# A state-space mixer and an MLP on one core: tap products of single channels for two of four channel groups

## The chip, the core and the metric

The kernel runs on one NeuronCore of a Trainium2 chip. The core has a matrix engine (PE, with its weight loads shown as PEld), two engines that work on elements (DVE and ACT), a general one (POOL) and a queue engine that starts transfers (SP); ACT starts transfers too. PE writes only to PSUM, eight banks of 512 fp32 columns, which DVE or ACT must copy out. The metric is device time in microseconds of one execution; lower is better.

## What is computed

The input is 2048 positions of 512 channels. A layer norm feeds a diagonal state-space layer, which is a long convolution along the positions, one kernel of 2048 taps for each channel; the result is added to the input. A second layer norm feeds an MLP with 1376 hidden units, and its result is added too. Cut to what matters here:

```
P = exp(logdA[:, :, None] * l[None, None, :])          # logdA = dt * (A_re + i A_im), 512 x 128
K = einsum("dn,dnl,dn->dl", Cc, P, dB).real            # the taps: 512 channels x 2048
y = irfft(rfft(pad(u)) * rfft(pad(K)))[..., :L]        # causal convolution
h = x + y + u * Dskip                                  # u = layernorm(x)
h2 = h + gelu(layernorm(layernorm(h)) @ w1 + b1) @ w2 + b2
```

The position index `l` is in bf16, so positions above 256 fall together on multiples of 2, 4 and 8. The kernel therefore needs the taps only at a few distinct positions, and writes each as a product of two powers: one of 20 rows (`ROWS`, `NA = 20`) times one of 33 columns (`NB = 33`).

## The kernel before

**Tables.** The 512 channels are four groups `c` of 128 (`CW`). For each group there are four tables in SBUF with the 128 states on the partitions: `EA[c]`, `IA[c]` (cosine and sine part of the row powers with the coefficients) and `EB[c]`, `IB[c]` (of the column powers). `bexps` and `aexps` make the magnitudes on ACT, `chain` and `chain1` the phases: PE sums them up in PSUM, ACT takes the sine (L1026, L1063), DVE multiplies (L1036, L1043, L1068). A table keeps four channels side by side, so neighbouring rows of one channel lie four elements apart. The row tables have 32 rows (`NP_`) for each channel, of which 20 are used; `gap` (L756) clears the other twelve.

**Tap products.** `kgen(c)` (L1075 to L1104) makes the taps. One product takes two channels at once: its stationary operand is 52 wide (32 rows of one channel, then 20 of the next), its moving operand is 66 wide (33 columns of each). Of the four blocks that come out, the two on the diagonal are the channels' own taps and the other two are not used. Two column tiles of the array, `t` = 0 and 1, hold channels of the two halves. For each of 32 steps `i` there are four products in the order tile 0 real, tile 0 imaginary, tile 1 real, tile 1 imaginary; the imaginary one is added to the real one in PSUM. Five blocks of steps (7, 7, 7, 7, 4) fill banks, and three copies (`evac`: L616 on ACT, L618 on DVE) bring them to SBUF, blocks 1 and 2 together, 3 and 4 together, and 5. A small add (L1104) puts in `Dskip`. A group has 128 products.

**After the taps.** `kspec` (groups 0 and 1 together), `kspec1` (groups 2 and 3, one by one) and `ktail` (late positions) multiply the taps into the first stage of a Fourier transform (L1120, L1145, L1166), copy them out, and turn them by a transfer to DRAM and back; `fstage` (L967) does the second stage. The input goes through `lnorm`, `austage` (L946) and `fstage` in the same way, for two halves of the positions, b = 0 and 1. `inverse` multiplies spectra on DVE (L1235) and transforms back on PE (L1245). `tail` adds the result to the residual (L1319, L1322), takes statistics (L1323, then small steps on DVE with a power on POOL, L689, L694) and normalises (L1334, L1336); a transpose on PE (L1346) or by transfer follows. `mlp` has two matmuls (L1362, L1378) with the GELU on ACT (L1364) between them and the last add on DVE (L1380), from which each tile goes out in two transfers of 64 partitions.

**The order.** Nothing is scheduled while the kernel runs: each engine works through its instructions in the order in which they were written, and waits where an operand is late. Every step is recorded as an operation with its engine, a cost and what it depends on. `ORDER` is a list of all of them, found by a search ahead of time: an entry is twice the operation's number, plus one where an operation that two engines can do is put on the second. A negative entry stands for four products that nobody reads. `SLOTS` gives the PSUM bank for each new PSUM tile in turn. The costs in the code serve that search and change nothing on the chip.

Of the kernel before, what the change touches and what calls it, by code (L numbers as in the profile page):

```python
# [15 lines left out]
P = 128  # L16
# [259 lines left out]
class VS(V):  # L276
# [51 lines left out]
]  # L328
SLOTS = "0124626046204620462406220246200626224606446426424602606426042060242042604206246240264024604620406240245651620426262341302560134076205472541326036260721452042067563414307136506437056253104574107423"


TURN = 450000


class Sched:
    def __init__(self):
        self.ops = []
        self.wr, self.rd = {}, {}
# [102 lines left out]
def kernel(ctx, tc, A_u, A_A_re, A_A_im, A_B_re, A_B_im, A_C_re, A_C_im, A_log_dt, A_Dskip,  # L441
# [963 lines left out]
    for c in (2, 3):  # L1405
        chain1(c, 5 + 0.25 * c)
        if c == 2:
            gap(IA[2:3], 5.95)
# [92 lines left out]
```

## Time and profile before

| | |
|---|---|
| three executions, median | 230.77 us (230.60 to 230.82) |
| the profiled execution, its own time | 230.71 us |
| its span, first to last instruction | 228.9 us |
| busy PE, DVE, ACT, POOL | 196.2, 173.5, 164.4, 14.6 us |
| L1092, tap products, 512 | 18.3 us, first at 57.1, last at 93.3 |

The page gives each engine's busy time and its share of the span, then the span in 40 slices of 5.7 us with the busy share of each in tenths, then the chain of work that ended last. Views of the trace group instructions by line and shape, cut the span into stretches, or list the instructions in order of time. In a group the columns are: line, engine, operation, output and input, shapes, count, busy time in us, mean length of one in ns, idle time of the engine ahead of them and what ended it. Matmuls overlap in the array, so the mean length of one (242 ns for L1092) is far above busy time over count.

### The profile page before, as it was taken

How to read it: one execution, taken by the hardware profiler on the slowest of the kernel's cores; microseconds unless marked ns; L12 is line 12 of the kernel's file. 1: busy time of each engine (PE TensorE's matmuls, PEld its weight loads, DVE VectorE, ACT ScalarE, POOL GpSimd, SP SyncE). 2: the span in 40 equal slices, each digit the busy share in tenths (PEclk: the TensorE clock that was granted, in tenths of full speed). 3: DMA queues.
4: the chain of work that ended last, by engine and by line, in shares of the span. 5: the costliest groups of instructions: out<-in, count | busy, mean ns of one | idle time of the engine just before them, and what ended most of it. 6: DMA issues, size and time to landing. Idle time of an engine off the chain costs nothing.

```text
span 228.9 us, 6859 instructions
## 1 busy us (share of the span) xinstructions
PE 196.2 (86%) x2974; PEld 113.6 (50%) x2981; DVE 173.5 (76%) x279; ACT 164.4 (72%) x203; POOL 14.6 (6%) x26
## 2 busy tenths in 40 slices
PE   7113886776999899999999769999999999999993
PEld 4102752233874479756566446654444434444452
DVE  7999778999897995779899989899957467113022
ACT  4999999999888997998997598593325405803800
POOL 2000300300010001200000030300000101000000
PEclk9999999999999999999999999999999999999998
DMA  5970191153006955486698991019340142051202
GB/s 154 191 145 6 53 234 41 51 159 127 6 3 118 227 145 146 131 180 158 175 243 164 258 227 67 3 33 218 72 93 21 29 101 69 11 126 44 63 21 70
DMA packets 43159, 25.09 MB, mean 110 GB/s; under 512 B 30197, under 2 KB 40697, under 8 KB 43130
## 3 DMA queue, kind: packets, MB, share of 16 engines
q1 hardware_dynamic: 41576, 22.72, 44.2%
q10 hardware_dynamic: 1554, 1.93, 2.7%
q8 instruction: 23, 0.38, 0.7%
q14 instruction: 6, 0.05, 0.1%
HBM read 14.13 MB, written 5.28 MB: 85 GB/s over the span
## 4 chain that ended last, share of the span: by engine, by line
PE 53%; ACT 26%; DVE 10%; DMA 4%; issue 4%; POOL 1%; ACTq 0%; SPq 0%; DVEq 0%; POOLq 0%
PE ps L1362 17%; PE ps L1378 17%; ACT ar L616 8%; PE ps L1092 7%; ACT ar L793 7%; ACT ar L1063 5%; ACT ar L991 4%; PE ps L1245 4%; DVE ar L1235 2%; DMA HL_d<-ar 2%; PE ps L946 2%; DMA ar<-AKc_d 2%; DVE ar L971 1%; DVE ar L1068 1%; ACT ar L701 1%
## 5 line engine op out<-in xcount | busy, mean ns | idle before, releaser
L616 ACT CAST ar<-ps 128x1024 bf16<-128x1024 f32 (+3 forms) x73 | 62.4, 917 | 10.8 <-PE ps L1245 5.3
L1364 ACT ACTIVATE ar<-ps,ar 128x512 bf16<-128x512 f32 (+1 forms) x44 | 27.6, 685 | 34.1 <-PE ps L1362 28.6
L1362 PE MATMUL ps<-ar 128*128 128x512 bf16 (+1 forms) x176 | 40.1, 379 | 0.1
L1378 PE MATMUL ps<-ar 128*128 128x512 bf16 (+3 forms) x181 | 39.8, 366 | 0.3
L1380 DVE TENSOR_TENSOR ar<-ps,ar 128x512 bf16<-128x512 f32 (+1 forms) x17 | 10.6, 652 | 26.7 <-issue 19.7
L1378 PEld LDWEIGHTS <-ar 128*128 128x128 bf16 (+1 forms) x187 | 17.9, 98 | 19.7 <-issue 0.7
L1362 PEld LDWEIGHTS <-ar 128*128 128x128 bf16 (+1 forms) x176 | 17.3, 100 | 20.2 <-issue 0.5
L618 DVE CAST ar<-ps 128x1024 bf16<-128x1024 f32 (+4 forms) x18 | 19.5, 1091 | 6.6 <-PE ps L1092 2.5
L1235 DVE TENSOR_TENSOR ar<-ar 128x2048 bf16<-128x2048 bf16 x20 | 24.0, 1218 | 0.5 <-ACT ar L616 0.3
L1245 PE MATMUL ps<-ar 64*128 64x128 bf16 x672 | 21.5, 216 | 1.9 <-DVE ar L1235 1.5
L1245 PEld LDWEIGHTS <-ar 64*128 64x128 bf16 x672 | 19.1, 94 | 6.5 <-issue 3.2
L1063 ACT ACTIVATE ar<-ps 128x1024 bf16<-128x1024 int16 x20 | 19.5, 1037 | 1.6 <-PE ps L1061 1.4
L1092 PE MATMUL ps<-ar 128*52 128x66 bf16 x512 | 18.3, 242 | 0.4 <-DVE ar L1068 0.4
L689 POOL TENSOR_TENSOR ar<-ar 128x4 f32<-128x4 f32 (+1 forms) x6 | 9.5, 1577 | 143.3 <-DVE ar L694 104.6
L1092 PEld LDWEIGHTS <-ar 128*52 128x52 bf16 x512 | 16.8, 128 | 2.7 <-issue 1.8
L946 PE MATMUL ps<-ar 128*32 128x512 bf16 x256 | 16.4, 381 | 1.0 <-DVE ar L931 0.9
L1026 ACT ACTIVATE ar<-ps 128x1024 bf16<-128x1024 int16 x16 | 15.9, 1035 | 0.4 <-PE ps L1018 0.3
L793 ACT ACTIVATE ar<-ar 128x1024 bf16<-128x1024 f32 x16 | 15.6, 1044 | 0.6 <-DVE ar L675 0.6
L1061 PE MATMUL ps<-ar 128*32 128x256 f16 (+1 forms) x256 | 12.9, 301 | 3.0 <-ACT ar L1063 2.8
L694 DVE SCALAR_TENSOR_TENSOR ar<-ar 128x4 f32<-128x4 f32 (+3 forms) x33 | 9.9, 305 | 6.4 <-POOL ar L689 5.4
L967 PE MATMUL ps<-ar 128*64 128x128 bf16 (+2 forms) x160 | 13.6, 298 | 0.9 <-ACT ar L616 0.9
L1068 DVE TENSOR_TENSOR ar<-ar 128x1024 bf16<-128x1024 bf16 x20 | 12.9, 682 | 0.6 <-ACT ar L1063 0.4
(83 smaller groups left out, 229.0 us busy)
## 6 DMA issues: line engine op xcount, KB each, us to landing
ar<-in_A_u_dram SPq DMA_DIRECT2D x16, 128.0 KB
ar<-in_A_u_dram SPq DMA_DIRECT2D x8, 256.0 KB
out_dram<-ar SPq DMA_DIRECT2D x30, 64.0 KB
ar<-in_B_w_dram SPq DMA_DIRECT2D x3, 344.0 KB
AK_d<-ar SPq DMA_DIRECT2D x2, 512.0 KB
AKc_d<-ar SPq DMA_DIRECT2D x4, 256.0 KB
ar<-tab_TP SPq DMA_DIRECT2D x1, 768.0 KB
ar<-AKc_d SPq DMA_DIRECT2D x3, 256.0 KB
```

The costliest lines, as they stand in the source:

```text
L616: act.copy(out_fn(), in_fn())
L618: dve.tensor_copy(out_fn(), in_fn())
L793: add("ACT", c_act(1024) + 0.03, lambda e, e0=e0: act.activation(free(EB0 // 2 + 4 * (16 - e0), [[8 * e0, 2], [4 * NB, NCH * CW // 4], [1, ...
L946: pe.matmul(pst(p)[32 * j:32 * j + 32, 512 * z:512 * z + 512], lhsT=BX.ap()[:, f0 + z, 16 - 16 * c:48 - 16 * c], rhs=src[2 * j + c].ap(), ...
L1026: add("ACT", c_act(1024), lambda e, p=p, sc=sc, cs=cs: act.activation(sc[cs].ap().rearrange("p c e d -> p (c e d)").rearrange("p (x e f) - ...
L1063: add("ACT", c_act(1024), lambda e, sc=sc: act.activation(sc.ap().rearrange("p z a b -> p (z a b)").rearrange("p (x a f) -> p a x f", a=4, ...
L1092: pe.matmul(o, lhsT=free(ta.lo // 2 + q * 4 * NP_ + f, [[4, NP_ + NA]]), rhs=free(tb.lo // 2 + q * 4 * NB + f, [[4, 2 * NB]]), start=ta is ...
L1235: dve.tensor_tensor(pq.ap().rearrange("p n d -> p (n d)"), a, b_, ALU.mult)
L1245: pe.matmul(pst(p)[:, 512 * h + 128 * k:512 * h + 128 * k + 128], lhsT=q.ap()[rows, x, :], rhs=TP[w].ap()[rows, f0 // 2 + k, :], start=(n ...
L1362: pe.matmul(pst(p)[:fs], lhsT=w1s[dc].ap()[:, fc * P:fc * P + fs], rhs=ybuf.ap().rearrange("p (t c) k -> p c t k", c=4)[:, dc], start=(dc ...
L1364: add("ACT", c_act(512, 1), lambda e, p=p, fc=fc, fs=fs: act.activation(hT.ap()[:fs, fc, :], pst(p)[:fs], ACT.Gelu_apprx_tanh, bias=b1_sb. ...
L1378: pe.matmul(pst(p)[:, c0:c1], lhsT=hT.ap()[:fs, fc, 128 * t:128 * t + 128], rhs=w2s[fc].ap()[:fs, c0:c1], start=(fc == 0), stop=(fc == NFC ...
```

## The change

For groups 0 and 1 the tap products stay those of two channels, but they go through the array in turn: the loop over the tiles `t` is inside that over the real and imaginary part, so the order is tile 0 real, tile 1 real, tile 0 imaginary, tile 1 imaginary.

For groups 2 and 3 a product takes one channel: 20 wide in the stationary operand and 33 in the moving one. Four column tiles `g` of 32 are used in turn, eight products a step, 256 a group. No unused blocks come out, so PSUM holds half as much: three blocks of steps (11, 11, 10) and two copies, of 726 and 330 elements for each partition, in place of three of 924, 924 and 264. The tap buffers `kgc` are half as large, `kspec1` and `ktail` read them without the index of the two channels, and the unused rows of `EA[2]`, `EA[3]` and `IA[2]` need no clearing: one `gap` on DVE and one on POOL go.

With that the program has 902 recorded operations instead of 914, and `ORDER` and `SLOTS` are new from the first entry to the last.

```diff
 ORDER = [
-    2, 0, 52, 4, 58, 54, 56, 50, 62, 154, 6, 64, 66, 68, 74, 82, 8, 102, 104, 12, 10, 136, 194, 14, 140, 106, 88, 108, 16, 24, 32, 118, 100, 60, 28,
...
-    1814, 1820, 1822, 1826, 1824,
+    52, 0, 6, 2, 50, 4, 8, 12, 10, 56, 62, 292, 22, 60, 152, 64, 100, 190, 66, 72, 84, 98, 14, 94, 134, 102, 58, 104, 16, 70, 162, 106, 116, 90, 68,
...
+    1798, 1800, 1802, 1774, 1758, 1752, 1776, 1784, 1786, 1778, 1788, 1760, 1790, 1762, 1764, -7, 1766,
 ]
...
-    kgc = [at(lo, bf16, 2, NB, 32) for lo in (xall.lo + 10240, K0)]
+    kgc = [at(lo, bf16, NB, 32) for lo in (xall.lo + 10240, K0)]
...
     gap(EA[0:2], 0, "DVE")
-    gap(EA[2:4], 0, "DVE")
...
-    KIS = [[(0, 7), (7, 7)], [(14, 7), (21, 7)], [(28, 4)]]
+    KIS2 = [[(0, 7), (7, 7)], [(14, 7), (21, 7)], [(28, 4)]]
+    KIS1 = [[(0, 11), (11, 11)], [(22, 10)]]
+    two = (0, 1)
...
-                    def fn(e, p=p, nb=nb, i0=i0, lo=lo, hi=hi):
+                    def fn2(e, p=p, nb=nb, i0=i0, lo=lo, hi=hi):
                         for i in range(lo, hi):
-                            for t in range(2):
-                                q, f = 16 * t + 2 * ((i0 + i) // 4), (i0 + i) % 4
-                                o = pst(p)[64 * t:64 * t + 32 + NA, 512 * nb + 2 * NB * i:512 * nb + 2 * NB * i + 2 * NB]
-                                for ta, tb in ((Ar, Br), (Ai, Bi)):
-                                    pe.matmul(o, lhsT=free(ta.lo // 2 + q * 4 * NP_ + f, [[4, NP_ + NA]]), rhs=free(tb.lo // 2 + q * 4 * NB + f, [[4, 2 * NB]]), start=ta is Ar, stop=ta is Ai, tile_position=(0, 64 * t))
-                    add("PE", 0.064 * (hi - lo), fn, r=[Ar, Br, Ai, Bi], w=[p], new=[p] if first else [])
+                            for ta, tb in ((Ar, Br), (Ai, Bi)):
+                                for t in range(2):
+                                    q, f = 16 * t + 2 * ((i0 + i) // 4), (i0 + i) % 4
+                                    o = pst(p)[64 * t:64 * t + 32 + NA, 512 * nb + 2 * NB * i:512 * nb + 2 * NB * i + 2 * NB]
+                                    pe.matmul(o, lhsT=free(ta.lo // 2 + q * 4 * NP_ + f, [[4, NP_ + NA]]), rhs=free(tb.lo // 2 + q * 4 * NB + f, [[4, 2 * NB]]), start=ta is Ar, stop=ta is Ai, tile_position=(0, 64 * t), skip_group_check=True)
+
+                    def fn1(e, p=p, nb=nb, i0=i0, lo=lo, hi=hi):
+                        for i in range(lo, hi):
+                            for ta, tb in ((Ar, Br), (Ai, Bi)):
+                                for g in range(4):
+                                    q, f = 16 * (g // 2) + 2 * ((i0 + i) // 4) + g % 2, (i0 + i) % 4
+                                    o = pst(p)[32 * g:32 * g + NA, 512 * nb + NB * i:512 * nb + NB * i + NB]
+                                    pe.matmul(o, lhsT=free(ta.lo // 2 + q * 4 * NP_ + f, [[4, NA]]), rhs=free(tb.lo // 2 + q * 4 * NB + f, [[4, NB]]), start=ta is Ar, stop=ta is Ai, tile_position=(0, 32 * g), skip_group_check=True)
+                    add("PE", (0.064 if Z == 2 else 0.074) * (hi - lo), fn2 if Z == 2 else fn1, r=[Ar, Br, Ai, Bi], w=[p], new=[p] if first else [])
...
-        add("DVE", c_dve(64), lambda e: dve.tensor_tensor(ks()[:, :, 0], ks()[:, :, 0], Dz.ap()[:, c, :].unsqueeze(1).to_broadcast([P, 2, 32]), ALU.add), r=[kg, Dz], w=[kg])
+        if Z == 2:
+            add("DVE", c_dve(64), lambda e: dve.tensor_tensor(ks()[:, :, 0], ks()[:, :, 0], Dz.ap()[:, c, :].unsqueeze(1).to_broadcast([P, 2, 32]), ALU.add), r=[kg, Dz], w=[kg])
+        else:
+            add("DVE", c_dve(32), lambda e: dve.tensor_tensor(ks()[:, 0], ks()[:, 0], Dz.ap()[:, c, :], ALU.add), r=[kg, Dz], w=[kg])
...
     for c in (2, 3):
         chain1(c, 5 + 0.25 * c)
-        if c == 2:
-            gap(IA[2:3], 5.95)
```

More of the change, by code (lines that the diff above doesn't have):

```diff
@@ L292 @@
 ORDER = [
[35 rows of a table removed]
[34 rows of a table added]
 ]
-SLOTS = "0124626046204620462406220246200626224606446426424602606426042060242042604206246240264024604620406240245651620426262341302560134076205472541326036260721452042067563414307136506437056253104574107423"
+SLOTS = "01426060264062402460202046022460606024202462442620402640202406264206426042604204624064026042642064023602546047020202637260670613216270324165464674304620431463172506156323475041273641671651307452"
 TURN = 450000
@@ L1078, in kgen @@
         kg = Kg[0] if c < 2 else kgc[c - 2]
-        ks = (lambda: kg.ap()[:, :, :, c]) if c < 2 else kg.ap
+        Z = 2 if c in two else 1
+        ks = (lambda: kg.ap()[..., c, :]) if c < 2 else kg.ap
+        KIS = KIS2 if Z == 2 else KIS1
         for grp in KIS:
@@ L1098, in ofn @@
             def ofn(i0=i0, n=n, N=N):
-                return ks().rearrange("p z k i -> p (z k) i")[:, :, i0:i0 + n * N].rearrange("p q (b i) -> p q b i", b=N)
+                a = ks()
+                if Z == 2:
+                    a = a.rearrange("p z k i -> p (z k) i")
+                return a[:, :, i0:i0 + n * N].rearrange("p q (b i) -> p q b i", b=N)
             def ifn(p=p, n=n, N=N):
-                return pst(p).rearrange("p (b q) -> p b q", b=N)[:, :, 0:2 * NB * n].rearrange("p b (i q) -> p q b i", q=2 * NB)
-            evac(ofn, ifn, 2 * NB * n * N, [p], [kg])
-        add("DVE", c_dve(64), lambda e: dve.tensor_tensor(ks()[:, :, 0], ks()[:, :, 0], Dz.ap()[:, c, :].unsqueeze(1).to_broadcast([P, 2, 32]), ALU.add), r=[kg, Dz], w=[kg])
+                return pst(p).rearrange("p (b q) -> p b q", b=N)[:, :, 0:Z * NB * n].rearrange("p b (i q) -> p q b i", q=Z * NB)
+            evac(ofn, ifn, Z * NB * n * N, [p], [kg])
+        if Z == 2:
+            add("DVE", c_dve(64), lambda e: dve.tensor_tensor(ks()[:, :, 0], ks()[:, :, 0], Dz.ap()[:, c, :].unsqueeze(1).to_broadcast([P, 2, 32]), ALU.add), r=[kg, Dz], w=[kg])
+        else:
+            add("DVE", c_dve(32), lambda e: dve.tensor_tensor(ks()[:, 0], ks()[:, 0], Dz.ap()[:, c, :], ALU.add), r=[kg, Dz], w=[kg])
     def kspec(q, pr):
@@ L1144, in mm @@
                         oo = pst(ps[g // 2])[:, 512 * (g % 2) + 256 * cp:512 * (g % 2) + 256 * cp + 256].rearrange("p (k i) -> p k i", k=8)
-                        pe.matmul(oo, lhsT=W.ap()[rows, tl, P * v:P * v + P], rhs=kg.ap()[rows, g % 2, k0:k0 + 8, :], start=(m == 0), stop=(m == len(js) - 1), tile_position=(32 * g, 0))
+                        pe.matmul(oo, lhsT=W.ap()[rows, tl, P * v:P * v + P], rhs=kg.ap()[rows, k0:k0 + 8, :], start=(m == 0), stop=(m == len(js) - 1), tile_position=(32 * g, 0))
             add("PE", 0.45 * (1 + cp), mm, r=[kg, W], w=ps, new=ps if cp == 0 else [])
@@ L1156, in ktail @@
         al = ALb[q]
-        kk = (lambda x: Kg[0].ap()[:, :, :, x]) if q == 0 else (lambda x: kgc[x].ap())
+        kk = (lambda x, z: Kg[0].ap()[:, z, :, x]) if q == 0 else (lambda x, z: kgc[x].ap())
         S.pr = pr
@@ L1165, in mm @@
                         rows = slice(32 * g, 32 * g + NA)
-                        pe.matmul(pst(ps[g // 2])[32 * x:32 * x + 32, 512 * (g % 2):512 * (g % 2) + 32 * NJ].rearrange("p (j i) -> p j i", j=NJ), lhsT=W1.ap()[rows, tl, :], rhs=kk(x)[rows, g % 2, 8 * tl:8 * tl + NJ, :], start=(tl == 0), stop=(tl == 3), tile_position=(32 * g, 32 * x))
+                        pe.matmul(pst(ps[g // 2])[32 * x:32 * x + 32, 512 * (g % 2):512 * (g % 2) + 32 * NJ].rearrange("p (j i) -> p j i", j=NJ), lhsT=W1.ap()[rows, tl, :], rhs=kk(x, g % 2)[rows, 8 * tl:8 * tl + NJ, :], start=(tl == 0), stop=(tl == 3), tile_position=(32 * g, 32 * x))
         add("PE", 1.15, mm, r=([Kg[0]] if q == 0 else kgc) + [W1], w=ps, new=ps)
```

65 rows, old and new, of the table ORDER are left out of this document.

## The prediction

> **What bounds the kernel now.** I read the page first: the span, the busy shares, the forty slices, the chain that ended last.
>
> ```profile
> span 228.9 us, 6859 instructions
> PE 196.2 (86%) x2974; PEld 113.6 (50%) x2981; DVE 173.5 (76%) x279; ACT 164.4 (72%) x203; POOL 14.6 (6%) x26
> ...
> PE   7113886776999899999999769999999999999993
> ...
> DVE  7999778999897995779899989899957467113022
> ACT  4999999999888997998997598593325405803800
> ...
> PE 53%; ACT 26%; DVE 10%; DMA 4%; issue 4%; POOL 1%; ACTq 0%; SPq 0%; DVEq 0%; POOLq 0%
> ```
>
> The first ten slices belong to ACT, the last sixteen mostly to PE; between them all three engines are near full. So I cut the span where the chain changes hands: at 57.1 the first tap products start, at 83.9 DVE ends the last table product of group 3, at 133.9 the statistics of the first second-half tile row are done, at 225.4 PE has finished. Columns are the length of the stretch, then busy time and instructions of PE, PEld, DVE, ACT, POOL.
>
> ```profile
> 0.00:57.10 57.10, 34.06 (x580) 19.00 (x581) 51.20 (x86) 53.45 (x60) 5.71 (x18) 1.00 0.47 116
> 57.10:83.90 26.80, 25.71 (x618) 16.87 (x620) 24.52 (x35) 24.68 (x30) 0.89 (x2) 1.00 0.45 93
> 83.90:133.90 50.00, 46.51 (x1138) 32.95 (x1134) 43.05 (x70) 42.20 (x50) 4.09 (x3) 1.00 0.79 186
> 133.90:225.40 91.50, 89.88 (x655) 44.77 (x655) 54.29 (x89) 44.09 (x67) 3.94 (x3) 1.00 0.33 70
> ```
>
> After 133.9 PE idles 1.6 us in 91.5: whatever PE work is left at that point is the rest of the run. So two things decide: when the statistics at 133.9 come (call it the anchor), and how much PE work still stands behind them.
>
> **The tap products.** Half of the change is here. Columns: group, count, busy, mean of one. Then stretches that hold one line's products alone.
>
> ```profile
> L1092 PE MATMUL ps<-ar 128*52 128x66 bf16 x512 | 18.3, 242 | 0.4 <-DVE ar L1068 0.4
> ```
> ```profile
> 85.20:89.20 4.00, 4.00 (x130) 3.89 (x124) 1.00 0.35 80
> ```
> ```profile
> L967 PE MATMUL ps<-ar 128*64 128x128 bf16 x16 | 0.6, 222 | 0.0
> ```
> ```profile
> 105.55:105.97 0.42, 0.42 (x16) 0.42 (x16) 1.00 0.81 271
> ```
> ```profile
> 100.86:101.27 0.41, 0.41 (x32) 0.37 (x32) 1.00 0.58 3
> ```
>
> The first stretch is L1092: 4.00/130 = 30.8 ns a product, so a group of 128 costs 3.94 us of PE. The second is L967, two column tiles in turn, 128 columns: 0.42/16 = 26 ns. The third is L1166, 288 columns on sixteen tiles: 0.41/32 = 13 ns.
>
> *Turning the order over the two tiles (groups 0 and 1).* One L1092 product takes 242 ns and one leaves every 30.8, so they overlap already: in tile order 0,0,1,1 the second product on tile 0 can run beside the first on tile 1. In order 0,1,0,1 each tile still gets every second product. I price this at nothing; the ends are 0 and the gain of a pair costing what its columns cost in L967 (66/128 of 52 = 27 ns instead of 61.6: 256 products save 4.4 us of PE). I stay at nothing since PE's tiles are equally loaded either way.
>
> *Single channels (groups 2 and 3).* Before, 128 products of 66 columns on two tiles; after, 256 of 33 columns on four. If four run abreast and cost goes by columns, four take half a pair, 30.8 ns, 7.7 each: 256 x 7.7 = 2.0 us. If only two run abreast, 15.4 each, 3.9 us: no gain. L1166 at 13 ns (3.3 us) carries far more columns, L1092 scaled is the nearest row; I take 9 ns, 2.3 us. PE saves 2 x (3.94 - 2.3) = 3.3 us; ends 0 and 3.9.
>
> The Trainium skill, "TensorE: Matmul & The Clock Gate", section "Wait — 56ns, not 53.3ns?", says that start to start never drops below about 25 ns however few the columns. By it 256 products would take 6.4 us, an estimate from that page, and the change would add PE time. The 13 ns of L1166 contradict it for products on different tiles. The same page, "LDWEIGHTS (loading the stationary operand)", has a load last columns/1.2 ns; four loads of 20 in a row would be 67 ns by it and eat the whole gain. Two loads of 52 would be 87 ns a pair, and the pair takes 61.6 here, so loads of different tiles overlap.
>
> **Evacuations and clears.** Each of groups 2 and 3 had three copies out of PSUM (924, 924, 264 elements) and now has two (726, 330).
>
> ```profile
> L616 ACT CAST ar<-ps 128x1024 bf16<-128x1024 f32 x51 | 49.7, 1027 | 8.5 <-PE ps L1245 5.3 <-PE ps L946 1.5 <-PE ps L1187 1.2
> ...
> L618 DVE CAST ar<-ps 128x1024 bf16<-128x1024 f32 x10 | 12.0, 1219 | 2.4 <-ACT ar L991 1.2 <-PE ps L967 0.9 <-PE ps L1120 0.3
> ...
> L616 ACT CAST ar<-ps 128x924 bf16<-128x924 f32 x5 | 4.6, 936 | 1.0 <-PE ps L1092 1.0
> ...
> L618 DVE CAST ar<-ps 128x924 bf16<-128x924 f32 x3 | 3.4, 1118 | 2.5 <-PE ps L1092 2.5
> ...
> L756 DVE MEMSET ar<- 128x1536 f32 x2 | 2.7, 1338 | 0.5 <-issue 0.5
> ...
> L616 ACT CAST ar<-ps 128x264 bf16<-128x264 f32 x4 | 1.5, 380 | 1.0 <-PE ps L1092 1.0
> ```
>
> Between these rows 726 elements cost about 0.78 on ACT and 330 about 0.45: 1.2 in place of 2.2, so 2 us less over both groups. One DVE clear of 1.34 goes, early, where ACT sets the pace: worth nothing. One POOL clear goes, and POOL is idle.
>
> **The new order.** An entry of the list is twice the operation's number, plus one for the second engine; with twelve operations gone the numbers can be matched and the two lists compared engine by engine.
>
> *To the first product.* ACT carries the same work ahead of the last sine of group 0: four copies of 1024 come in, four leave. I leave 57.1.
>
> *57.1 to 83.9.* ACT gets one copy of 924 and one of 726 more and one of 576 less: 0.92 + 0.78 - 0.65 = 1.05 us (576 by the same rows). PE gets four operations of group 2 (22 x 8 products at 9 ns, 1.6) and loses the tail spectrum (one L1166 stretch, 0.4): 1.2 more. ACT idles 2.1 and PE 1.1 there by the stretch above. I take +0.8; ends 0 and +1.2.
>
> *83.9 to the anchor.* On DVE come in four copies of 1024, three small ones, two spectrum products, two residual adds; out go three copies of 1024 and one of 512, one normalisation and one statistics.
>
> ```profile
> L1235 DVE TENSOR_TENSOR ar<-ar 128x2048 bf16<-128x2048 bf16 x20 | 24.0, 1218 | 0.5 <-ACT ar L616 0.3
> ...
> L923 DVE BATCH_NORM_STATS2 ar<-ar 128x6 f32<-128x512 bf16 x16 | 10.0, 674 | 0.0
> ...
> L931 DVE TENSOR_SCALAR ar<-ar 128x512 bf16<-128x512 bf16 x16 | 5.6, 406 | 0.1
> ...
> L1322 DVE TENSOR_TENSOR ar<-ps,ar 128x512 bf16<-128x512 f32 x12 | 7.8, 680 | 6.6 <-issue 3.6 <-PE ps L1319 3.0
> ...
> L618 DVE CAST ar<-ps 128x512 bf16<-128x512 f32 x2 | 1.4, 692 | 1.7 <-PE ps L1145 1.7
> ```
>
> In: 4 x 1.2 + 2 x 0.7 + 0.45 + 2 x 1.2 + 2 x 0.65 = 10.35. Out: 3 x 1.2 + 0.7 + 0.35 + 0.6 = 5.25. DVE must do 5.1 more, 48.1 in a stretch of 50.0 in which it idled 6.95. Where did it idle?
>
> ```profile
> 83.90:94.50 10.60, 10.58 (x302) 9.55 (x297) 7.07 (x19) 8.67 (x12) 2.16 (x2) 1.00 0.47 135
> ```
>
> Half of it, 3.5, while PE was full with the products of groups 2 and 3. In the new list eight of the twenty product operations no longer exist, four stand earlier and the rest are cheaper, so this wait should mostly go. I leave DVE 1.9 idle: the stretch stays 50.0. Ends: 49 (idle 0.9) and 55 (all idle kept).
>
> *Behind the anchor.* Four PE operations leave this part and are done ahead of it: one inverse product of 64, two residual products, one transpose group.
>
> ```profile
> 143.42 1.89 PE ps L1245 x64
> ...
> 179.92 0.34 PE ps L1319 x2
> ```
> ```profile
> L1346 PE MATMUL ps<-ar 128*128 128x128 bf16 x16 | 1.4, 220 | 0.1
> ```
>
> 1.89 + 2 x 0.34 + 1.4/4 = 2.9 us less of what nothing else covers. That is where the 3.3 us of the products go: filler moves forward into them.
>
> *The end.* Before, the last add is of 256 columns and its two transfers go out on SP and ACT. Now the last PE work is a whole tile, and both its transfers stand on SP.
>
> ```profile
> 225.39 0.42 DVE L1380 TENSOR_TENSOR ar<-ps,ar 128x256 bf16<-128x256 f32 x1 [0.52 <-PE ps L1378]
> ```
> ```profile
> L1380 DVE TENSOR_TENSOR ar<-ps,ar 128x512 bf16<-128x512 f32 x15 | 9.7, 683 | 24.3 <-issue 19.7 <-PE ps L1378 4.4 <-DMA out_dram<-ar 0.2
> ```
> ```profile
> 221.67 4.98 SPq L632 DMA_DIRECT2D out_dram<-ar  x7
> ```
>
> 0.68 - 0.42 = 0.26 more, and a second issue behind the first (4.98/7 = 0.7 a place, of which the old last one also waited about half): +0.5. Ends 0.2 and 1.0. The fill products that end PE's list have no reader. Nine transfer issues change between SP and ACT, five to SP and four to ACT; I price that, like the new PSUM banks, at nothing: a late bank or transfer would show as a wait of PE and cost what it lasts.
>
> **The sum.** The profiled execution took 230.71 (span 228.9 and 1.8 around it), the median of three is 230.77. 230.7 + 0.8 + 0.0 - 2.9 + 0.5 = 229.1; I forecast **229.1**.
>
> **Rivals.** *DVE becomes the bound of the middle (slower).* It has 5.1 us more between 83.9 and the anchor. The other terms sum to -1.6, so from 3.5 us of remaining idle (stretch 51.6) the kernel is no faster, and beyond it slower; with all 6.95 kept the time is 230.7 + 0.8 + 5.1 - 2.9 + 0.5 = 234.2, with two thirds kept 231.9. For it: from 116 on DVE's slices are 9 already and its copies are dearer than ACT's (1.2 against 0.97). Against it: half the idle waits on PE work that goes. 0.23.
>
> *The turned order speeds groups 0 and 1 too.* 4.4 us off PE between 57 and 69, slices full for PE but also 8 and 9 for ACT and DVE, which leave 1 to 2 us: 227.5. For it: a pair of 66 columns now costs more than a pair of 128 in L967. Against: the overlap that is there already. 0.12.
>
> *The narrow products don't run four abreast* (the change doesn't do what it says): at 15.4 ns PE gains nothing, the fillers can't move, 229.1 + 3.3 = 232.4. A start floor as on the page would do the same and more: were each product to keep L1092's 30.8 ns, PE would gain 7.9 us and the time pass 240. The page for this is the Trainium skill's, named above; the 13 ns speak against. 0.09 together.
>
> **How the numbers follow.** Forecast 0.56, rivals 0.23, 0.12, 0.09. The range takes in the turned order with a luckier anchor below (225.9) and the two slower rivals up to about two thirds of DVE's idle kept and the unsplit gain above (232.4); beyond lie about 0.1 on each side at most. A measurement tells 0.2%, 0.46 us, from no change. Faster: the forecast but 0.02, and the turned order, 0.66. Same: 0.02 and the edges of the slower rivals, 0.10. Slower: 0.24.
>
> **What would show it.** Products of 66 columns still at about 31 ns each and those of 33 at 9, 256 in 2.3 us; DVE idle between group 3's last table product and the last statistics step behind POOL's pow at 2 us or less; PE busy behind that point about 87 instead of 89.9, hardly any idle; last add to end of span 0.5 longer than 3.5. It is wrong if the anchor lies past 136, or if the 33-column products take over 15 ns.

## The result, and the profile after

The changed kernel is slower, by 1.7%.

| | before | changed |
|---|---|---|
| median of four executions | 230.76 us (230.60 to 230.82) | 235.01 us (234.80 to 235.10) |
| ratio | | 1.0168, 95% interval 1.0147 to 1.0189 |
| profiled execution, time and span | 230.71, 228.9 us | 234.94, 233.2 us |

The forecast was 229.1 with a range of 225.9 to 232.4, so the sign is wrong too. All medians and ratios below leave out the slow executions, such as one of the changed kernel of 323 us. The lines of the code have moved: L1092 is now L1094 (pairs) and L1102 (single channels), L616 and L618 are L615 and L617, L946 and L967 are L944 and L965, L1061 is L1059, L1120 and L1145 are L1136 and L1161, L1235 is L1251, L1245 is L1261, L1380 is L1396. First the page of the changed kernel, the rows that answer to those shown of before:

```profile
span 233.2 us, 7372 instructions
...
PE 197.9 (85%) x3241; PEld 110.3 (47%) x3241; DVE 173.6 (74%) x281; ACT 161.6 (69%) x198; POOL 13.8 (6%) x25
...
PEclk9999999999999999999999988999999999999999
...
q8 instruction: 25, 0.41, 0.8%
```

PE has 267 products more and 1.7 us more busy time. Two rows are new to the argument. The granted clock dips in two slices, between 134 and 146 us. And there is a queue that brings instructions (packets, MB, share of the DMA engines): 25 packets, 0.41 MB, so 16 KB each, against 6482 products and weight loads on PE, about 256 a packet. (The kernel before has 23 packets for 5955.) Next the windows, cut where those of before were cut: at the first tap product, at the end of a table product of group 3, at the anchor (the statistics of the first second-half row) and at PE's end. The table product is in both kernels the last but one; the last ends at 84.5 before and at 86.8 now.

```profile
56.66:85.50 28.84, 25.35 (x804) 17.07 (x808) 24.25 (x34) 24.36 (x28) 0.00 (x0) 1.00 0.33 58
85.50:138.50 53.00, 46.99 (x1232) 29.68 (x1218) 47.79 (x76) 43.05 (x50) 4.01 (x3) 1.00 0.70 172
138.50:229.10 90.60, 89.86 (x627) 45.02 (x623) 51.97 (x89) 40.75 (x63) 3.94 (x3) 0.98 0.34 83
```

From the first product to PE's end it is 172.4 us now and was 168.3. Busy PE time in it is 162.2 (before 162.1), so the 4.1 us show as idle PE (behind the equal sums stand 2.5 us less in the product rows, 18.3 before and 9.4 + 6.4 now, and as much more in other rows, 1.1 of it from a halved clock, below). The start is 0.4 sooner, the stretch behind PE's end 4.1 in place of 3.5 us: -0.4 + 4.1 + 0.6 = 4.3, the difference of the spans. The groups of PE by shape tell where the idle time is (line, shapes, count, busy, mean ns of one, idle ahead of them and what ended it):

```profile
L1094 PE MATMUL ps<-ar 128*52 128x66 bf16 x256 | 9.4, 243 | 0.0
...
L1102 PE MATMUL ps<-ar 128*20 128x33 bf16 x512 | 6.4, 200 | 2.9 <-issue 2.9
```

In the kernel before, the pairs of groups 2 and 3 alone have this row:

```profile
L1092 PE MATMUL ps<-ar 128*52 128x66 bf16 x256 | 9.1, 242 | 0.0
```

The turned pairs cost what they cost (256 in 9.4 us, before 512 in 18.3). The single channels are busy for 6.4 us and idle for 2.9, together 9.3 against 9.1 for the pairs, so nothing is saved. "Issue" says that nothing that the profile shows held them. In order of time on PE (start, length, line, count; in brackets the idle time ahead):

```profile
75.84 0.80 PE L1102 MATMUL ps<-ar 128*20 128x33 bf16 x70
77.00 0.34 PE L1102 MATMUL ps<-ar 128*20 128x33 bf16 x18 [0.36 <-issue]
77.28 0.62 PE L965 MATMUL ps<-ar 128*64 128x512 bf16 x4
77.83 0.62 PE L1059 MATMUL ps<-ar 128*32 128x512 f16 x8
78.27 1.04 PE L944 MATMUL ps<-ar 128*32 128x512 bf16 x16
79.14 0.90 PE L1102 MATMUL ps<-ar 128*20 128x33 bf16 x82
81.00 0.24 PE L1102 MATMUL ps<-ar 128*20 128x33 bf16 x6 [0.97 <-issue]
81.05 0.63 PE L1059 MATMUL ps<-ar 128*32 128x256 f16 x16
81.62 1.04 PE L1136 MATMUL ps<-ar 20*128 20x512 bf16 x16
83.02 0.62 PE L1059 MATMUL ps<-ar 128*32 128x256 f16 x16 [0.36 <-ACT ar L1061]
83.46 0.83 PE L1102 MATMUL ps<-ar 128*20 128x33 bf16 x74
85.01 0.24 PE L1102 MATMUL ps<-ar 128*20 128x33 bf16 x6 [0.72 <-issue]
...
89.01 0.59 PE L1102 MATMUL ps<-ar 128*20 128x33 bf16 x46 [0.89 <-issue]
...
93.02 0.83 PE L1161 MATMUL ps<-ar 20*128 20x256 bf16 x22 [0.20 <-issue]
...
97.02 0.84 PE L965 MATMUL ps<-ar 128*64 128x512 bf16 x10 [0.53 <-issue]
```

Count the products from one gap to the next, whatever line they have: 18 + 4 + 8 + 16 + 82 = 128 from 77.00 to the gap at 80, and 6 + 16 + 16 + 16 + 74 = 128 from 81.00 to the gap at 84. The same 128 lie between 85.01, 89.01, 93.02 and 97.02, and there the gap falls on products of other lines too. Each product is two instructions with its weight load, so PE stops every 256 instructions, and starts again every 4.0 us. A wait for a bank or for a copy would not keep that count. That gave the theory to test: **the supply of instructions** on PE is a limit of its own. The Trainium skill, "Advanced Engine Details and Errata", section "ISA Cache", has a cache line of 16 KB, which is 256 instructions; packets and gaps here agree with it. (No run here has products without a load of their own, so 128 products and 256 instructions aren't told apart by the gaps alone.) How long a line takes to come is what the runs below show.

### The profile page after: what moved, and what is told of

The parts are those of the page before. It is cut to its first block, busy times and chain, and to the rows that moved or that the text cites. A ratio compares the mean times of both kernels' runs of the same rounds, so it can differ in the third digit from the quotient of the medians.

```text
span 233.2 us, 7372 instructions
## 1 busy us (share of the span) xinstructions
PE 197.9 (85%) x3241; PEld 110.3 (47%) x3241; DVE 173.6 (74%) x281; ACT 161.6 (69%) x198; POOL 13.8 (6%) x25
## 4 chain that ended last, share of the span: by engine, by line
PE 67%; ACT 25%; DVE 3%; issue 3%; POOL 0%; ACTq 0%; DVEq 0%; POOLq 0%
PE ps L1394 17%; PE ps L1378 16%; PE ps L1261 9%; ACT ar L791 7%; ACT ar L615 5%; PE ps L944 5%; PE ps L965 4%; ACT ar L989 4%; PE ps L1094 4%; ACT ar L1061 3%; PE ps L1059 3%; ACT ar L1024 3%; PE ps L1102 2%; DVE ar L1251 2%; PE ps L1016 2%
## 5 line engine op out<-in xcount | busy, mean ns | idle before, releaser
L615 ACT CAST ar<-ps 128x1024 bf16<-128x1024 f32 (+5 forms) x69 | 61.0, 920 | 13.3 <-PE ps L1261 6.0
L1380 ACT ACTIVATE ar<-ps,ar 128x512 bf16<-128x512 f32 (+1 forms) x44 | 27.8, 689 | 35.7 <-PE ps L1378 35.5
L1394 PE MATMUL ps<-ar 128*128 128x512 bf16 (+3 forms) x187 | 40.7, 367 | 0.0
L1396 DVE TENSOR_TENSOR ar<-ps,ar 128x512 bf16<-128x512 f32 (+1 forms) x17 | 10.9, 656 | 28.3 <-PE ps L1394 28.3
L1261 PE MATMUL ps<-ar 64*128 64x128 bf16 x672 | 23.1, 225 | 2.6 <-ACT ar L615 1.6
L1251 DVE TENSOR_TENSOR ar<-ar 128x2048 bf16<-128x2048 bf16 x20 | 23.8, 1220 | 2.0 <-PE ps L1261 1.8
L617 DVE CAST ar<-ps 128x1024 bf16<-128x1024 f32 (+6 forms) x20 | 20.6, 1033 | 6.1 <-PE ps L1161 2.2
L1261 PEld LDWEIGHTS <-ar 64*128 64x128 bf16 x672 | 20.6, 99 | 7.6 <-DVE ar L1251 4.5
L1061 ACT ACTIVATE ar<-ps 128x1024 bf16<-128x1024 int16 x20 | 19.8, 1051 | 3.2 <-issue 1.3
L944 PE MATMUL ps<-ar 128*32 128x512 bf16 x256 | 17.4, 381 | 2.0 <-DVE ar L929 1.7
L965 PE MATMUL ps<-ar 128*64 128x512 bf16 (+2 forms) x160 | 14.4, 299 | 1.4 <-DVE ar L617 0.5
L1059 PE MATMUL ps<-ar 128*32 128x256 f16 (+1 forms) x256 | 13.0, 301 | 3.0 <-ACT ar L1061 2.9
L1338 DVE TENSOR_TENSOR ar<-ps,ar 128x512 bf16<-128x512 f32 x12 | 8.0, 683 | 6.1 <-ACT ar L1380 4.9
L863 PE MATMUL ps<-ar 128*32 128x256 f16 x32 | 3.0, 413 | 10.9 <-DMA ar<-tab_I 6.0
```

The source lines that it names most:

```text
L615: act.copy(out_fn(), in_fn())
L617: dve.tensor_copy(out_fn(), in_fn())
L944: pe.matmul(pst(p)[32 * j:32 * j + 32, 512 * z:512 * z + 512], lhsT=BX.ap()[:, f0 + z, 16 - 16 * c:48 - 16 * c], rhs=src[2 * j + c].ap(), ...
L965: pe.matmul(pst(p)[64 * h:64 * h + 64, w * (k + r):w * (k + r) + w], lhsT=T.ap()[:, f, r, :], rhs=v[f:f + 1].ap()[:, 0, :], start=True, st ...
L1061: add("ACT", c_act(1024), lambda e, sc=sc: act.activation(sc.ap().rearrange("p z a b -> p (z a b)").rearrange("p (x a f) -> p a x f", a=4, ...
L1251: dve.tensor_tensor(pq.ap().rearrange("p n d -> p (n d)"), a, b_, ALU.mult)
```

## The experiments

Each time is the median of the executions, the ratio is to the kernel before on the same chip, with its 95% interval.

### Products by themselves

A kernel of its own, each set behind 28 products of 512 columns.

```diff
+ for n in range(128):                 # set 4, single channels
+     for im in range(2):
+         for g in range(4):
+             matmul(20 x 33, operands at a step of four elements, column tile g)
```

(This cut is in short form.)

> A kernel of its own with nothing but products, each set behind 28 products of 512 columns: 512 pairs (52x66) in the old tile order, 512 in turn, 512 in turn with neighbouring operands, 1024 single channels (20x33) on four tiles, 1024 of them with neighbouring operands, 512 of 128 columns on two tiles. Theory A, the supply of instructions is the limit (256 instructions, 128 products with their weight loads, about every 4.0 us): after a quick start every set settles at 30 to 32 ns a product, whatever its shape, stride and tile order; 1024 single channels take about 30 us. Theory B, the prediction's (tiles overlap, cost goes by columns): single channels stay at 9 to 10 ns, 1024 in about 10 us, and 512 pairs need 15 to 16 us. Theory C, the stride of the operands is the limit: sets 3 and 5 are clearly quicker than 2 and 4.

In order of time on PE; L42 and L49 are pairs in the old and the new tile order, L56 pairs with operands side by side, L63 single channels:

```profile
19.97 16.39 PE L42 MATMUL ps<-tb,ta 128*52 128x66 bf16 x512
...
42.44 16.32 PE L49 MATMUL ps<-tb,ta 128*52 128x66 bf16 x512
...
64.84 4.18 PE L56 MATMUL ps<-tb,ta 128*52 128x66 bf16 x259
69.78 2.16 PE L56 MATMUL ps<-tb,ta 128*52 128x66 bf16 x128 [0.76 <-issue]
...
97.37 1.28 PE L63 MATMUL ps<-tb,ta 128*20 128x33 bf16 x128 [2.18 <-issue]
100.83 1.29 PE L63 MATMUL ps<-tb,ta 128*20 128x33 bf16 x128 [2.18 <-issue]
```

Single channels run in bursts of exactly 128, 10 ns each, and then stand still for 2.2 us: 3.46 us from one burst to the next, or 27 ns a product. With operands side by side they do the same, with 3.45 to 4.00 us from burst to burst. So theory A is right for them, with a smaller number than I gave it (27, not 30 to 32), and theory B holds only inside a burst. For pairs it is wrong: they take 31.9 ns in either tile order without one gap, which the supply would allow, and 16.1 ns (4.18/259) with operands side by side, until supply gaps appear there as well. What limits the pairs is the step of their operands (theory C). The array isn't what the single channels wait for either, as two windows show, one burst at whole and one at half the granted clock (length, PE, PEld, DVE, POOL, then the clock):

```profile
87.00:88.30 1.30, 1.29 (x128) 1.18 (x128) 0.00 (x0) 0.00 (x0) 1.00 0.05 13
...
100.83:102.12 1.29, 1.29 (x128) 1.16 (x128) 0.00 (x0) 0.00 (x0) 0.50 0.05 13
```

128 products take 1.29 us at both clocks, so inside a burst the clock of the array doesn't set the pace either.

A second kernel of this kind took the operands and the mixture apart.

> A kernel of its own with products alone, like the first. Sets: 256 pairs with only the stationary operand strided, 256 with only the moving one strided, 256 with both at a step of two, 128 times one product of 512 columns and seven single channels behind it, 256 single channels all on one tile, 1024 single channels on four tiles beside 2 MB of transfers. Supply theory: where long products lie between the single channels the demand is below one block of 128 products in 3.5 us, so the fourth set has gaps of no more than a few tenths of a microsecond and lasts about 128 x (0.22 + 7 x 0.0095) = 37 us; the last set keeps its bursts of exactly 128 and its period is 3.5 us or longer. Rival (the gaps belong to the single-channel products themselves): the fourth set has gaps of 2 us after every 128 single channels. On the pairs: about 16 ns where the operand that costs lies side by side, about 32 where it is strided.

```profile
L66 PE MATMUL ps<-tb,ta 128*20 128x33 bf16 x256 | 8.8, 199 | 0.0
L50 PE MATMUL ps<-tb,ta 128*52 128x66 bf16 x256 | 8.1, 241 | 0.0
L46 PE MATMUL ps<-tb,ta 128*52 128x66 bf16 x256 | 6.6, 216 | 0.0
L54 PE MATMUL ps<-tb,ta 128*52 128x66 bf16 x256 | 4.5, 196 | 0.0
```

Pairs cost 31.6 ns with only the moving operand at a step of four (L50), 25.8 with only the stationary one (L46), and 17.6 with both at a step of two (L54). Single channels on one tile take 34.4 ns (L66) and on four 10, so they do run four abreast. The single channels beside transfers kept their bursts of 128, 3.45 to 4.28 us apart. The set with long products between had no gap of 2 us, as supply has it, but lasted 63 us instead of 37, which neither theory had. Its first round, and its last with the product that follows it:

```profile
57.08 0.38 PE L58 MATMUL ps<-tb,ta 128*128 128x512 bf16 x1
57.38 0.24 PE L61 MATMUL ps<-tb,ta 128*20 128x33 bf16 x7
57.56 0.39 PE L58 MATMUL ps<-tb,ta 128*128 128x512 bf16 x1
...
119.65 0.39 PE L58 MATMUL ps<-tb,ta 128*128 128x512 bf16 x1
119.97 0.24 PE L61 MATMUL ps<-tb,ta 128*20 128x33 bf16 x7
120.14 3.19 PE L31 MATMUL ps<-tb,ta 128*128 128x512 bf16 x13
```

128 rounds from 57.08 to 120.14 are 0.49 us each, not the 0.29 expected: some 0.2 us a round are lost where PE passes from the whole array to tiles and back. (The Trainium skill, "TensorEngine Tiling (Array Packing)", "Key Properties", says that a change of the tiling mode drains the array; this trace agrees, but no run tells a drain from the weight loads that go with the change.)

### The turned order alone, for all four groups

```diff
-                            for t in range(2):
-                                for ta, tb in ((Ar, Br), (Ai, Bi)):
+                            for ta, tb in ((Ar, Br), (Ai, Bi)):
+                                for t in range(2):
```

> The kernel before with the loop over the two tiles inside that over real and imaginary part, for all four groups; all else as it was. Supply theory and the prediction's step alike: pairs stay at 30 to 31 ns, time 230.8 within 0.5. Rival (two tiles in turn run abreast): pairs near 15 ns, time 227 to 229.

230.72 us, ratio 0.9997 (0.9980 to 1.0014). The group L1092 has the same row as before. Turning does nothing.

### Single channels alone, in the order of the kernel before

```diff
-    KIS = [[(0, 7), (7, 7)], [(14, 7), (21, 7)], [(28, 4)]]
+    KIS2 = [[(0, 7), (7, 7)], [(14, 7), (21, 7)], [(28, 4)]]
+    KIS1 = KIS2
+    two = (0, 1)
...
+                    def fn1(...):        # as in the change: 20 x 33, four tiles
```

> The kernel before with its own order, banks and five blocks, but groups 2 and 3 as single channels on four tiles (256 products a group instead of 128, three copies of half the size). The prediction's price (9 ns, 2.3 us a group): PE saves 3.3 us, 1 to 3 us faster, 227.8 to 229.8. Supply theory: a group lasts 4.6 to 7.9 us in place of 3.9 wherever it runs in one go, with gaps every 128 products; the smaller copies give back up to 2 us; 230.5 to 234.

236.24 us, ratio 1.0233 (1.0179 to 1.0287), slower than either theory had; the changed kernel has 1.0135 (1.0093 to 1.0177) on this chip, below. All operations stand where they stood in the kernel before, so the delay can be read off: at the last copy of group 3 it is 4.0 us (98.3 against 94.25). It arises where the products are (PE in order of time):

```profile
84.64 1.09 PE L1104 MATMUL ps<-ar 128*20 128x33 bf16 x101
88.36 1.48 PE L1104 MATMUL ps<-ar 128*20 128x33 bf16 x128 [2.62 <-issue]
91.81 0.49 PE L1104 MATMUL ps<-ar 128*20 128x33 bf16 x35 [1.98 <-issue]
```

Here the products stand in one go, so the gaps are as long as in the kernel of products alone. Behind these two gaps DVE's copy starts 3.1 us late (92.28 against 89.14). The rest comes between 92 and 97, where the granted clock was 0.50 for most of the time, so it can't all be put down to the gaps. The new order of the changed kernel, which puts other work between the products, is better with them than the old one, not worse.

### Half of the instructions, and a quarter of the columns

```diff
-                            for ta, tb in ((Ar, Br), (Ai, Bi)):
+                            for ta, tb in ((Ar, Br),):
...
-                                    ..., start=ta is Ar, stop=ta is Ai, ...
+                                    ..., start=True, stop=True, ...
```

> The changed kernel with the imaginary products of groups 2 and 3 left out (128 single-channel products a group; the sine part of those taps is missing). Supply theory: the gaps of 0.4 to 1.0 us inside the product sets go almost wholly, both groups take about 2.5 us of PE instead of 9.3; the end comes 2 to 5 us sooner, 230 to 233. Rival (the gaps come from changes of bank or from waits for the copies): gaps stay at the same places between product operations, products take half, 3.2 us less PE, and the end moves by 0 to 2 us, 233 to 235. If the time stays at 235 within 0.5, the products have no part in the loss and the order around the anchor has it all.

```profile
L1102 PE MATMUL ps<-ar 128*20 128x33 bf16 x256 | 3.6, 200 | 0.5 <-issue 0.5
```

231.00 us, ratio 0.9978 (0.9952 to 1.0005). Three of the four gaps inside the product operations are gone, and the set takes 4.1 us where it took 9.3. That is more than the 2.5 expected, and about what the prediction had priced for all of them (4.6).

```diff
-    rhs=free(tb.lo // 2 + q * 4 * NB + f, [[4, NB]])
+    rhs=free(tb.lo // 2 + q * 4 * NB + f, [[4, 8]])
```

> The changed kernel with single-channel products of only the first 8 of the 33 columns (the other 25 columns of those taps are missing): as many instructions, a quarter of the columns. Supply theory: gaps at the same multiples of 128 products, both groups still take over 8.5 us, time within 1 us of the changed kernel. The prediction's pricing by columns (9 ns for 33): products go to 3 to 5 ns, both groups to 2 to 3 us, and the time falls like that of the run without imaginary products, by 3 to 4 us.

```profile
L1102 PE MATMUL ps<-ar 128*20 128x8 bf16 x512 | 5.8, 173 | 2.1 <-issue 2.0
```

232.95 us, ratio 1.0103 (1.0058 to 1.0148), against 233.99, ratio 1.0135 (1.0093 to 1.0177), for the changed kernel beside it. With a quarter of the columns both groups take 7.9 us, a little less than the 8.5 expected of the supply, and nowhere near 2 to 3. By the ratios, half of the instructions saved 3.6 us (1.0135 - 0.9978 of 231 us); three quarters of the columns saved 0.7 us, and there the intervals overlap. So instructions are what is paid for, and columns little if at all.

### The changed kernel again, and the clock

> The changed kernel once more, as the measure for the two runs beside it on the same chip: 235.0 within 0.5, about 1.017 of the kernel before. Granted clock below 1 for some microseconds behind the idle stretch around 136.

The ratio is 1.0135 (1.0093 to 1.0177), the median 233.99 us: it agrees with the first within the interval, but the profiled execution was at 233.56 us, with a span of 231.8. (PE's gaps come in it too, 3.45 to 4.55 us apart.) Windows of this execution and of the first, cut alike (length, PE, PEld, DVE, ACT, POOL, clock):

```profile
138.00:140.00 2.00, 1.64 (x60) 1.64 (x61) 1.96 (x4) 2.00 (x4) 0.18 (x1) 1.00 1.05 360
140.00:142.00 2.00, 1.92 (x28) 1.08 (x22) 2.00 (x4) 2.00 (x5) 0.00 (x0) 1.00 1.08 401
```
```profile
138.00:140.00 2.00, 1.64 (x32) 1.64 (x33) 1.96 (x4) 2.00 (x4) 0.18 (x1) 0.56 1.08 359
140.00:142.00 2.00, 2.00 (x42) 1.89 (x37) 0.70 (x3) 1.05 (x2) 0.00 (x0) 0.59 1.08 401
```

The anchor comes at 138.5 in both. Then the first has the clock at half for about 3.5 us and does 32 products where the second does 60. From 142 on it is 1.4 us behind, and ends so (span 233.2 against 231.8). So 1.4 of the 4.3 us in the first profile are a halved clock, which the same kernel has in one execution and not in another. The Trainium skill, "TensorE: Matmul & The Clock Gate", Part 1, has a gate that watches PE's activity over a window of about 3.4 us which runs freely, whatever the kernel does. No run here shows its length; that one kernel, idle at the same places, does both agrees with a window that runs freely. I tried to keep the clock with work that nobody reads, in PE's idle time between 132.8 and 137:

```diff
-    1100, 1010, 1032, 1338, 1040,
+    1100, -2, -2, -2, 1010, 1032, 1338, -2, -2, -2, -2, -2, 1040,
```

> The changed kernel with eight more fill operations (32 products that nobody reads) in the idle stretch of PE between 132.8 and 137. If the halved clock from 138 to 142 (1.6 us in the profile) comes from that idle stretch and adds to the end: 0.5 to 1.6 us less than the changed kernel on the same chip, the clock stays whole there. If the clock falls all the same, or the time isn't set there: no change within 0.5; the fills can cost at most their 1.7 us where they hold up other work.

234.51 us, ratio 1.0121 (1.0090 to 1.0152) beside 1.0135: nothing that can be told. Its own profile, of an execution of 234.72 us, had the clock whole behind 138, but it fell in two other slices (35 to 41 and 87 to 93 us), and the six executions went from 233.20 to 234.72. What decides where the clock falls isn't shown.

### The order by itself, and the end

The changed kernel's order with pairs for all groups; a third block of four operations and a copy are put into each of groups 2 and 3, where the list has free banks.

> The changed kernel's own order and banks, but the products of groups 2 and 3 as pairs again (turned, three blocks and three copies as before, the clears put back in); the extra block and copy of each group are put in where banks are free. If the single-channel products alone bring the loss: about what the first experiments leave, 229 to 230.8, not slower than the kernel before. If the new order has a loss of its own around the anchor (inverse products that wait ahead of the residual products): 232 to 234. The prediction's terms for the order alone (+0.8, -2.9, +0.5, and 3.3 more of PE work): 231 to 232.5.

240.57 us, ratio 1.0398 (1.0358 to 1.0437). This isn't a clean test of the order: among the products PE waits 3.3 us, in three places, for ACT to free a bank, two of them ahead of the blocks that I put in. It shows only that this order has no room for the third block. Together with the end put back:

> As the run before, but the last output tile is again the one in two halves of 256 columns, with transfers on both queues, as in the kernel before. The prediction's term for the end says 0.5 less than without it; ends 0.2 and 1.0. If the end is hidden: no change.

241.23 us, ratio 1.0409 (1.0376 to 1.0441), no gain. And the end put back in the changed kernel alone:

```diff
-    1782, 1798, 1800, 1802, 1774, 1758, 1752, 1776, 1784, 1786, 1778, 1788, 1760, 1790, 1762, 1764, -7, 1766,
+    1798, 1800, 1802, 1774, 1758, 1752, 1776, 1760, 1762, 1778, 1764, 1766, 1782, 1784, 1786, 1788, 1790, -7,
```

> The changed kernel with only the end of its order put back: the whole tile ahead, the tile in two halves last, its transfers on both queues. The prediction's term: 0.5 less (0.2 to 1.0), so 234.5; the traces' difference between last add and end of span gives 0.8, so 234.2.

234.35 us, ratio 1.0139 (1.0102 to 1.0176), beside 1.0168 and 1.0135 for the changed kernel. The intervals overlap; the half microsecond can't be told.

### Less work for DVE

With cheap products the changed order still only equals the kernel before. In the changed kernel's trace DVE's instructions follow each other almost without a gap from 104 to 139 (busy 34.7 of 35.0 us), so I took copies off it.

```diff
-    961, ... 875,
+    960, ... 874,
```

(For four copies 1295 and 751 become 1294 and 750 as well.)

> The changed kernel with two of the copies of 1024 columns at 106 and 114 us given back from DVE to ACT, as the kernel before had them: 2.4 us less for DVE, 2.0 more for ACT, the order as it is. If DVE sets the time from the last products to the anchor: 1 to 2.4 us less than the changed kernel (234.5 on this set of chips, 233.2 in executions with a whole clock). If PE sets it, or ACT is as full: within 0.5.

> The same two copies on ACT, with the imaginary products of groups 2 and 3 left out as before (the sine part of those taps is missing). If the products no longer hold the middle and DVE does: 1 to 2.4 us less than the 231.0 of the run with half the products, clearly below the kernel before. If ACT is as full: 230.5 to 231.5.

> Four copies back on ACT (105, 106, 107 and 114 us): 4.9 us less for DVE, 4 more for ACT, which idles 3.6 us between 100 and 127. If DVE alone sets the middle: 2 to 4 us less than the changed kernel. If ACT takes its place: no better than the run with two copies, or slower.

236.67, 234.30 and 238.12 us, ratios 1.0258 (1.0219 to 1.0296), 1.0109 (1.0071 to 1.0148) and 1.0278 (1.0240 to 1.0316): each slower than the same kernel without the exchange. In the first of them L582 is the copy and L911 a stage of the input's transform; of PE's waits behind 100 the longest is this one (total, times, longest):

```profile
PE ps L911 <- ACT ar L582: 2.3, 1, 2.3
```

Its window (length, PE, PEld, DVE, ACT, POOL, clock), that of the run with four copies, and then that of the changed kernel:

```profile
99.90:127.35 27.45, 24.75 (x534) 14.34 (x528) 20.59 (x25) 23.08 (x26) 0.00 (x0) 0.94 0.73 164
```
```profile
99.90:127.35 27.45, 23.98 (x540) 14.43 (x517) 18.93 (x24) 25.23 (x27) 0.00 (x0) 1.00 0.74 172
```
```profile
99.90:127.35 27.45, 26.97 (x626) 17.33 (x611) 26.38 (x33) 23.83 (x25) 0.00 (x0) 1.00 0.83 190
```

In the first of them all three engines do less in the same time, in part by a granted clock of 0.94. With four copies at a whole clock ACT does more, and PE and DVE do less: ACT comes to the copies later than DVE did, PE waits for the bank (2.3 and 2.1 us), and DVE for PE or for ACT (with four copies 6.5 us for ACT). A theory in which DVE alone sets the middle isn't borne out. PE at 98%, DVE at 96% and ACT at 87% are fitted to each other by this order. Which of them holds it where the products are cheap stays open.

## Why the prediction was wrong, step by step

**The single-channel products: the step that failed.** "I take 9 ns, 2.3 us. PE saves 2 x (3.94 - 2.3) = 3.3 us; ends 0 and 3.9." Both groups take 6.4 + 2.9 = 9.3 us, not 4.6. The pairs take 9.1 in the same kind of row, so instead of a saving of 3.3 us there is a loss of 0.2: the bad end of the term came true, and the term is off by 3.5 us. (The 7.9 that two groups of pairs have at 30.8 ns leave out the tail of each set, which the rows count.) The 9 ns were right for a product in a burst: 10 ns. What I left out is that twice the products are twice the instructions, and that each 256 of them take 3.45 us or more to come. The rows from which I scaled hid it: L967 with 16 products and L1166 with 32 are shorter than one block. And I scaled from pairs at 30.8 ns as if columns had set that price; the runs show the step of the operands there, at nearly the rate of the supply.

**The rival "narrow products not four abreast"** got 0.09. Its price of 15.4 ns is near the 18 that a product takes with its gaps (9.3/512), but its mechanism is wrong: they do run four abreast (34.4 ns on one tile, 10 on four). The floor of 25 ns from start to start that the Trainium skill has in "TensorE: Matmul & The Clock Gate", "Wait — 56ns, not 53.3ns?", doesn't hold across tiles here, as I said (10 ns in a burst). As a rate over hundreds of products by themselves 27 ns is what came out, for another reason.

**The rival "DVE becomes the bound of the middle"** got 0.23. Its time with all of DVE's idle kept, 234.2, is the nearest to the 235.0, and 5.2 of the 6.95 us of idle stayed. Its mechanism isn't shown: the runs that took copies off DVE put them on ACT and were slower, and between 99.9 and 127.35 PE is as full as DVE.

**The turned order at nothing**: right in size (0.9997), but not for the reason given. What sets the pace of the pairs in both orders is the step of their operands, which the prediction didn't have.

**Copies**: right. The four took 764, 915, 436 and 495 ns where I had 780 and 450 for ACT.

**57.1 to 83.9, +0.8**: the same point came at 85.5, +1.6; the gaps that end at 77, 81 and 85 lie ahead of it. It isn't the end of the last table product of group 3, as the prediction has it, but of the one before; the last moved by 2.3 us (84.5 to 86.8).

**83.9 to the anchor, 50.0**: 53.0. DVE's busy time was forecast well (48.1, measured 47.8). But of its idle time 5.2 us stayed, not 1.9, and 4.1 of that lies before 99.9 (14.4 - 10.3), mostly among the products: "this wait should mostly go" rested on the price above. (Whether it goes with cheap products isn't shown: with half of them the one profile has the clock at 0.76 just there.) So the signs that I named came true, anchor past 136 and products over 15 ns (18 with their gaps).

**Behind the anchor, -2.9**: 90.6 in place of 91.5 in the first profile, -0.9; with the whole clock 89.2, -2.3. That the moved work is worth about what it takes was right; the 1.4 us of halved clock weren't foreseen.

**The end, +0.5**: 0.8 in the trace, where the last add starts 4.3 us ahead of the end of the span (233.2) instead of 3.5; the timed runs don't tell it apart from nothing.

```profile
228.89 0.69 DVE L1396 TENSOR_TENSOR ar<-ps,ar 128x512 bf16<-128x512 f32 x1 [0.16 <-PE ps L1394]
```

Put together, between the first product and PE's end: forecast -2.1, measured +4.1. Of the 6.2 us of difference the products are 3.5 (time of PE, which need not all come out at the end) and the halved clock 1.4; the other 1.3 aren't taken apart. But this doesn't say that 9 ns would have brought 229.1. With half the instructions the products were cheaper than forecast (4.1 us, not 4.6), and the time was 231.00 beside 231.02 for the kernel before (ratio 0.9978, up to 1.0005): of 5.2 us of PE time 3.6 came out at the end. So the forecast that work moved forward fills all of the saving was too good as well, by 1.2 to 1.7 us (1.7 less forecast, 0 to 0.5 measured).

No version here is clearly faster than the kernel before. As an estimate from the runs above, a table with two channels side by side instead of four would bring pairs to 17.6 ns, where the supply would hold a long row of them at about 27; it wasn't tried.

## What to carry to other kernels

When a change makes matmuls smaller and more, count instructions as well as columns: ask how many fall into any 4 us of the engine's queue, and compare with 256. A price taken from a burst of 16 or 32 products says nothing of 500. Gaps that a profile puts down to "issue" are read by counting instructions from one to the next: if the count is always the same, whatever the line, it points to the supply. And operands with a step of four elements can double the price of a product.

## What the runs showed of the hardware that was not expected

- PE gets 256 instructions (128 products with their weight loads) every 3.45 to 4.0 us when it does nothing else, and every 4.0 us in the changed kernel (3.45 to 4.55 in its second profile).
- Products of 33 columns on four tiles take 10 ns each at half the granted clock as at the whole one.
- Pairs of 66 columns: 16.1 ns with operands side by side, 17.6 at a step of two elements, 31.9 at a step of four.
- In rounds of one product on the whole array and seven on tiles about 0.2 us a round are lost.
- One kernel has a halved clock for 3.5 us behind the same idle stretch in one execution and not in another, 1.4 us of the time.
